# A state-space mixer and a two-layer PReLU block on one core: chunk pair 1 in the half-partition layout, and another order in the first pairs and for the rows of the second half

## The chip, the core and the metric

The kernel runs on one core of one Trainium2 chip. A core has a matrix engine (TensorE, PE in the profile, with its weight loads as PEld), three engines for elementwise work (VectorE or DVE, ScalarE or ACT, GpSimd or POOL) and queues that issue transfers between the chip's outer memory and its inner one (here nearly all from SyncE's queue, SP). TensorE writes into eight banks of a small accumulation memory (PSUM); DVE and ACT can read those banks, POOL can't. The metric is the time of one execution in device microseconds; lower is better.

## The reference

A state-space layer (four batches, eight heads, 768 tokens, head size 32, state size 16) is followed by a two-layer block with PReLU. Cut to what matters:

```python
# for each batch and head, over chunks of the sequence (the result doesn't depend on the chunk's length)
cum = np.cumsum(log(clip(a)))                       # within the chunk
L   = exp(cum[i] - cum[j]) for i >= j, else 0
y   = ((C @ B.T) * L) @ x + (C @ state) * exp(cum)[:, None]
state = exp(sum(log a)) * state + (B * exp(cum[-1] - cum)[:, None]).T @ x
# then, on all 4 x 768 = 3072 tokens, with the heads side by side (256 wide)
h = y @ w_in                                        # 256 -> 2048
g = maximum(h, 0) + alpha * minimum(h, 0)
out = g @ w_out                                     # 2048 -> 256
```

The weights arrive as 64-bit floats and are turned into 32-bit ones on the chip.

## The kernel before, in words

**Chunks and pairs.** The kernel uses chunks of 128 tokens: 6 for each batch, 24 in all, worked on in 12 pairs (pair 0 is chunks 0 and 1 of batch 0, and so on). Four chunks (two pairs) make a group of 512 tokens, for which the two-layer block then runs; there are six groups.

**Two layouts.** Pairs 0 and 1 are done in `first_two` with a chunk's 128 tokens on the 128 partitions ("whole"). All later pairs put chunk k of a pair on half k of the partitions: 64 partitions hold the first 64 tokens and then the second 64 of that chunk. Since the decay matrix L is triangular, a head then needs 128 + 64 = 192 columns (`SQ`) instead of 256 for both chunks, and the matmuls run in smaller tiles of the array, more at once. The functions of this layout are `load_tokens` and `load_chunks` (loads), `turn_products` (transposes of B and C), `gram_products` (C times B), `scan_heads` (the decays), `decayed` (their product), `added` (the addition to the state), `x_products` and, inside `pair`, the products with the state. Because a chunk's state and C are needed on the other half of the partitions too, `moved_s` and `moved_c` hold copies of them moved across.

**Decays.** A decay matrix comes out of one scan on DVE for each stretch of columns: running product of the a values, with a one added at the diagonal (`ident_h`; for the half layout the bank `ident_p`, filled by `identity_bank`). For pairs 2 and later the a values are written out to memory as rows (`rows_clamp`, `rows_ends`, `rows_scan`, `rows_product`, `rows_out`), 96 rows for each half of the batches, and read back spread over the partitions (`load_spread`, tile `abc`). For pairs 0 and 1 the a values are spread on the chip, by matmuls with a column of the identity: `spread_rows` for pair 0 and `spread` for pair 1 (64x128 tiles), into the four PSUM banks `bank(0)` to `bank(3)`. `first_a` clamps them into the tile `z`.

**Weights.** Each matrix comes in eight pieces of 512 KB; the sixteen pieces are converted in the order in0, in1, in2, out0, in3, out1, in4 and so on. A conversion is: two steps on ACT (L263, and L270 or L273), one on POOL (L265), two on DVE (`sign` L284, L294) and one on POOL (L316). `convert_a` issues the ACT steps and L265, `convert_next` the rest. At most six raw pieces are held, so a load waits for an earlier piece's end.

**The first group** runs while the weights arrive. `hidden_two` does the first two pieces of w_in as soon as pair 0 and then pair 1 are done (L968), and from f = 4 to 15 `hidden` (L953, 128 hidden features by 512 tokens) alternates with `output` (L991). The result of a hidden product sits in one of two banks (`hp`); ACT multiplies it by alpha (L956) and DVE takes the maximum (L957), which frees the bank. Between these steps the stages of pairs 2 and 3 run (`ssm`, a generator with stages at fixed places): f = 4 to 9 has pair 2, f = 9 to 14 pair 3. Of `pair`'s stages the second calls `products_of_c` (cz on ACT, cd on POOL, then moved_c on ACT, L681), the fourth has the gram and the state.

**The order is written out by hand.** Every engine executes its instructions in the order in which the code issues them, so an instruction that waits holds up all later ones of its engine. SP's transfers too are issued in order: a, B, C and x of pair 0, a of pair 1, two weight pieces, the rows out (z, pf), pair 1's loads, weight pieces 2 and 3, pair 2's loads, weight pieces 4 and 5, abc of pair 2, then one piece for each one converted.

**The rest.** From the end of f = 15 on, the groups 1 to 5 run with seven products instead of eight for each block of two by two (`quad`, `product`, L1077 and L1052), and the remaining pairs run in between.

**What the change touches**, by line: the loads of the first pairs (`load_whole` L203, called at L225 and L851), the identity tiles (L330 to L332, `identity_bank` L387), `rows_ends` (L405), `pair_loads` (L468), `first_a` (L485), `spread` (L507), `pair` (moved_c at L680, state products at L725 to L734), `first_two` (L745 on, its own `mask`, `added`, `times`, `decays`, `outputs`), and the rows of the second half (L1289 to L1295).

Of the kernel before, what the change touches and what calls it, by code (L numbers as in the profile page):

```python
# [22 lines left out]
def kernel(  # L23
# [179 lines left out]
    def load_whole(gp):  # L203


        nat, _, xt, ap = pair_tiles(gp)
        b, c = divmod(2 * gp, CPB)
        if gp == 0:
            load_a(ap, b, c)
            load_rows(0, nc.scalar)  # L210
            nc.sync.dma_start(out=al_n, in_=moe_alpha.rearrange("(k p) -> k p", p=P))
        spans = [slice((c + k) * Q, (c + k + 1) * Q) for k in range(2)]
        for k, ts in enumerate(spans):
            for i, src in enumerate((B, C)):
                nc.sync.dma_start(out=nat[:, i, k].rearrange("p (h n) -> p h n", h=H),
                                  in_=src[b, :, ts, :].rearrange("h p n -> p h n"))
        for k, ts in enumerate(spans):
            nc.sync.dma_start(out=xt[:, k].rearrange("p (h d) -> p h d", h=H),
                              in_=x[b, :, ts, :].rearrange("h p d -> p h d"))
        if gp == 0:  # L220
            loads["a", 1] = prep.tile([P, 2 * Q], F32, name="a1")
            load_a(loads["a", 1], b, c + 2)

    al_n = const.tile([NF, P], F32, name="al_n")
    load_whole(0)  # L225
# [95 lines left out]
    def keep_warm(to, n, cols=2 * Q):  # L321

        for i in range(n):
# [6 lines left out]
    ident_h = const.tile([P, H * Q], F32, name="ident_h")  # L330
    nc.vector.tensor_copy(out=ident_h.rearrange("p (h t) -> p h t", h=H),
                          in_=ident.unsqueeze(1).to_broadcast([P, H, Q]))  # L332
# [54 lines left out]
    def identity_bank():  # L387
# [3 lines left out]
        nc.scalar.copy(out=m5_bank[0][:, HT:], in_=ident_h[:, :HT])  # L391
        for s in range(2):
            nc.scalar.copy(out=m5_bank[0][HQ:, HT:].rearrange("p (a s t) -> p s a t", a=2, s=2)[:, s],
                           in_=ident[HQ:, HQ * (1 - s) : HQ * (2 - s)].unsqueeze(1)
                           .to_broadcast([HQ, 2, HQ]))
# [9 lines left out]
    def rows_ends(i, eng=nc.vector):  # L405
        d0 = held[i]
        eng.tensor_copy(out=d0[:, Q + 1 :], in_=d0[:, HQ + 1 : Q])
# [60 lines left out]
    def pair_loads(gp):  # L468
# [6 lines left out]
        if gp >= NB:  # L475
# [9 lines left out]
    def first_a(ap, eng):  # L485

        z = prep.tile([P, 2, Q], F32, name="z", bufs=2)
        eng.memset(z[:, :, :1], 0.0)
        eng.tensor_scalar(out=z[:, :, 1:], in0=ap.rearrange("p (k t) -> p k t", k=2)[:, :, 1:],
# [17 lines left out]
    def spread(z, k, tile=lambda w: ss_tile()):  # L507

        ts = [tile(w) for w in range(2)]
        for q in range(4):  # L510
            for w in range(2):
                rs = slice(64 * w, 64 * w + 64)
                row = 64 * w + N * q
                nc.tensor.matmul(ts[w][:, q * Q : (q + 1) * Q],
                                 ident[rs, row : row + 1].to_broadcast([64, P]), z[rs, k],
                                 start=(q == 0), stop=True, tile_position=(64 * w, 0),
                                 skip_group_check=True)
        return ts
# [92 lines left out]

    def dps_of(gram):
# [8 lines left out]
    def pair(gp):  # L621
# [53 lines left out]
        def products_of_c():  # L675
            for e in range(2):
                nc.scalar.mul(cz[:, e].rearrange("p k t -> p (k t)"), ct, par[:, e : e + 1])
            nc.gpsimd.tensor_tensor(out=cd.rearrange("p k t -> p (k t)"), in0=ct, in1=pf,
                                    op=ALU.mult)
            for k, (to, frm) in enumerate(others):  # L680
# [6 lines left out]
        if fine:  # L687
            for i in range(4):
# [5 lines left out]
                if i == 3:  # L694
                    products_of_c()
                    move_states()
# [10 lines left out]
        if not fine:  # L707
# [3 lines left out]
            move_states()  # L711
        for i, r in enumerate((2, 3, 0, 1) if fine else (3, 2, 1, 0)):
# [12 lines left out]
        for i in range(2):  # L725
            for q in range(4):
                qs = slice(32 * q, 32 * q + 32)
                for k in range(2):
                    ks, w = slice(HQ * k, HQ * (k + 1)), k ^ i
                    if st[k] is not None:  # L730
                        nc.tensor.matmul(y[k][qs, w], (moved_s if i else st[k])[ks, qs],  # L731
                                         moved_c[ks] if i else cd[ks, k], start=i == 0,
                                         stop=False, tile_position=(HQ * k, 32 * q),
                                         skip_group_check=True)  # L734
# [10 lines left out]
    def first_two():  # L745
# [4 lines left out]
        dec = [work.tile([P, 2, H, Q], F32, name="dec") for i in range(2)]  # L750
        first = dec[0].rearrange("p a b t -> p (a b t)").rearrange(
# [18 lines left out]
        def gram_of(bc, cz, banks):  # L770
            gram = [t.rearrange("p (k h t) -> p k h t", k=2, h=2) for t in banks]
            for k in range(2):
                for r in range(4):
                    rs = slice(32 * r, 32 * r + 32)
                    nc.tensor.matmul(gram[r][:, k].rearrange("p h t -> p (h t)"), bc[rs, k],
                                     cz[rs, :, k], start=True, stop=True,
                                     tile_position=(32 * r, 0), skip_group_check=True)
            return gram

        def added(dps, bn, xt):  # L780
# [8 lines left out]
        def mask(sm, new, ks):  # L789
            n = ks.stop - ks.start  # L790
            nc.gpsimd.tensor_tensor(
                out=sm.rearrange("p k (g m) -> p k g m", g=2),
                in0=new[:, ks].unsqueeze(2).to_broadcast([P, n, 2, 2 * D]),
                in1=hmask.rearrange("p (g m) -> p g m", g=2).unsqueeze(1)
                .to_broadcast([P, n, 2, 2 * D]), op=ALU.mult)

        def copied(gram):
            g0 = op.tile([P, GT], F32, name="o_sb").rearrange("p (k h t) -> p k h t", k=2, h=2)
            nc.scalar.copy(out=g0, in_=gram)
            return g0  # L800

        def times(i, r, gram, eng=nc.vector):
            o = dec[1][:, :, 2 * r : 2 * r + 2] if i else by_bank[:, r]
            eng.tensor_tensor(out=o, in0=gram, in1=o, op=ALU.mult)

        def decays(k, w, t):
            ws = slice(512 * w, 512 * w + 512)
            nc.vector.tensor_tensor_scan(out=dec[1][:, k].rearrange("p h t -> p (h t)")[:, ws],
                                         data0=t, data1=ident_h[:, ws], initial=0.0,
                                         op0=ALU.mult, op1=ALU.add)  # L810

        def outputs(i, tiles, st, cd, xt, ws, warm=0):
            y = [t[:, : 2 * Q].rearrange("p (k t) -> p k t", k=2) for t in tiles]
            keep_warm(y[ws[0]].rearrange("p k t -> p (k t)"), warm)
            begun = False
            for k in range(2):
                if st[k] is None:
                    continue
                for q in range(4):
                    qs = slice(32 * q, 32 * q + 32)  # L820
                    for w in range(KC):
                        hs = slice(64 * w, 64 * w + 64)
                        nc.tensor.matmul(y[w][qs, k], st[k][hs, qs], cd[hs, k],
                                         start=not begun, stop=False,
                                         tile_position=(64 * w, 32 * q), skip_group_check=True)
                begun = True
            for w in ws:
                for k in range(2):
                    for q in range(4):
# [3 lines left out]
                                         dec[1][:, k, h] if i else by_bank[:, h // 2, k, h % 2],  # L833
                                         start=False, stop=True, tile_position=(0, 32 * q),
                                         skip_group_check=True)
                nc.scalar.copy(out=xts[0][:, w, 2 * i * Q : 2 * (i + 1) * Q],
# [561 lines left out]
```

## Time and profile before

| | |
|---|---|
| runs before: median of 7 (lowest to highest) | 363.3 us (361.7 to 363.69) |
| the profiled execution: its time, its span | 363.32 us, 361.6 us |
| busy over the span: PE, PEld, DVE | 352.7, 290.5, 233.6 us |
| busy over the span: ACT, POOL | 175.8, 209.6 us |
| mean granted clock of TensorE | 0.995 |
| transfers | 29.18 MB, 101422 packets |
| L529, decays of a head in the half layout (DVE, 128x192) | 80 x 526 ns |
| L808, decays of pair 1 (DVE, 128x512) | 4 x 1208 ns |
| L953, hidden of the first group (PE, 128x512) | 48 instructions, 22.7 us |

The 32-bit matmuls of TensorE appear as two instructions each. A matmul's busy time overlaps that of the next, so a busy PE isn't a PE at its peak. The chain of waits follows the work that ended last back to its cause; its pieces are told by the engine and line that each was spent on, and "issue" is time in which the engine waited for nothing that the profile shows. The page's chain has 86% of the span on PE.

The first 84 us are the first group and its weights; the span's slices show TensorE busy to eight tenths or more in all but the last slice (each digit is a fortieth of the span):

```profile
PE   8989999899999999999999999999999999999996
DVE  6797796778845647866656856657856634643363
ACT  3467854744455345545445545445545444443431
POOL 4586668589857847545546545537535545434521
```

### The profile page before, as it was taken

How to read it: one execution, taken by the hardware profiler on the slowest of the kernel's cores; microseconds unless marked ns; L12 is line 12 of the kernel's file. 1: busy time of each engine (PE TensorE's matmuls, PEld its weight loads, DVE VectorE, ACT ScalarE, POOL GpSimd, SP SyncE). 2: the span in 40 equal slices, each digit the busy share in tenths (PEclk: the TensorE clock that was granted, in tenths of full speed). 3: DMA queues.
4: the chain of work that ended last, by engine and by line, in shares of the span. 5: the costliest groups of instructions: out<-in, count | busy, mean ns of one | idle time of the engine just before them, and what ended most of it. 6: DMA issues, size and time to landing. Idle time of an engine off the chain costs nothing.

```text
span 361.6 us, 8061 instructions
## 1 busy us (share of the span) xinstructions
PE 352.7 (98%) x3128; PEld 290.5 (80%) x3128; DVE 233.6 (65%) x467; ACT 175.8 (49%) x399; POOL 209.6 (58%) x229
## 2 busy tenths in 40 slices
PE   8989999899999999999999999999999999999996
PEld 7766667467888788888888888888888888888884
DVE  6797796778845647866656856657856634643363
ACT  3467854744455345545445545445545444443431
POOL 4586668589857847545546545537535545434521
PEclk9899999999999999999999999999999999999999
DMA  6888979742748581401452442541001001002004
GB/s 109 166 177 206 336 123 292 109 89 49 140 98 152 93 137 21 89 2 23 86 99 31 89 88 32 94 84 29 1 4 29 0 2 29 2 1 32 0 1 87
DMA packets 101422, 29.18 MB, mean 81 GB/s; under 512 B 79928, under 2 KB 97288, under 8 KB 101384
## 3 DMA queue, kind: packets, MB, share of 16 engines
q1 hardware_dynamic: 100456, 28.43, 39.3%
q8 instruction: 24, 0.39, 0.5%
q10 hardware_dynamic: 928, 0.25, 0.3%
q14 instruction: 14, 0.11, 0.1%
HBM read 25.27 MB, written 3.39 MB: 79 GB/s over the span
## 4 chain that ended last, share of the span: by engine, by line
PE 86%; POOL 4%; DVE 4%; ACT 3%; issue 2%; POOLq 0%; ACTq 0%; DVEq 0%
PE bank L1052 33%; PE hp L1077 28%; PE ss L1077 5%; PE bank L991 4%; PE hp L953 3%; PE ss L606 2%; PE ss L586 2%; PE hp L968 2%; PE hp L324 2%; PE ss L731 1%; POOL wt L265 1%; DVE gt L957 1%; POOL w_out L316 1%; ACT wt L263 1%; POOL w_in L316 1%
## 5 line engine op out<-in xcount | busy, mean ns | idle before, releaser
L1134 POOL TENSOR_TENSOR gt<-gt 128x512 f32<-128x512 f32 x58 | 73.7, 1270 | 20.9 <-DVE gt L1062 16.1
L1052 PE MATMUL bank<-gt,w_out 128*128 128x256 f32 x320 | 83.6, 382 | 0.0
L1052 PEld LDWEIGHTS bank<-gt,w_out 128*128 128x128 f32 x320 | 60.1, 190 | 9.2 <-issue 1.0
L1124 POOL TENSOR_TENSOR gt<-gt 128x512 f32<-128x512 f32 x20 | 25.4, 1270 | 63.0 <-DVE gt L1062 53.6
L1062 DVE SCALAR_TENSOR_TENSOR gt<-hp,s_mul,gt 128x256 f32<-128x256 f32 x96 | 42.0, 479 | 29.7 <-ACT gt L1060 24.8
L1052 PE MATMUL bank<-gt,ws 128*128 128x256 f32 x240 | 59.5, 379 | 0.0
L1060 ACT ACTIVATE gt<-hp,s_alpha 128x256 f32<-128x256 f32 x96 | 40.3, 471 | 32.1 <-PE hp L1077 31.0
L1052 PEld LDWEIGHTS bank<-gt,ws 128*128 128x128 f32 x240 | 45.6, 190 | 6.2
L1077 PE MATMUL hp<-xs,w_in 128*128 128x256 f32 x160 | 41.9, 384 | 0.0
L1077 PE MATMUL hp<-xs,ws 128*128 128x256 f32 x160 | 41.1, 379 | 0.4 <-DVE gt L957 0.4
L529 DVE TENSOR_TENSOR_SCAN dec<-abc,bank 128x192 f32<-128x192 f32 x80 | 37.8, 526 | 2.7 <-DMA abc<-z 2.7
L1103 DVE TENSOR_TENSOR hp<-hp,u 128x512 f32<-128x512 f32 x20 | 14.0, 698 | 35.2 <-ACT u L1101 35.2
L1077 PEld LDWEIGHTS hp<-xs,ws 128*128 128x128 f32 x160 | 30.3, 190 | 4.9 <-POOL xs L1032 0.8
L1077 PEld LDWEIGHTS hp<-xs,w_in 128*128 128x128 f32 x160 | 29.7, 190 | 4.4
L991 PE MATMUL bank<-w_out,gt 128*128 128x256 f32 x128 | 30.8, 382 | 0.0
L991 PEld LDWEIGHTS bank<-w_out,gt 128*128 128x128 f32 x128 | 23.8, 190 | 6.5 <-issue 3.0
L1077 PE MATMUL ss<-xT,w_in 128*128 128x256 f32 x96 | 24.6, 379 | 0.0
L953 PE MATMUL hp<-xT,w_in 128*128 128x512 f32 x48 | 22.7, 596 | 0.5 <-DVE gt L957 0.4
L571 POOL TENSOR_TENSOR sm<-state,bmask 128x256 f32<-128x256 f32 (+1 forms) x10 | 6.4, 641 | 27.9 <-DVE state L644 27.9
L1092 ACT COPY m<-hp 128x512 f32<-128x512 f32 x8 | 4.7, 586 | 35.4 <-PE hp L1077 35.4
L1101 ACT COPY u<-hp 128x512 f32<-128x512 f32 x20 | 11.7, 585 | 19.9 <-PE hp L1077 19.9
L1062 DVE SCALAR_TENSOR_TENSOR gt<-c,s_mul,gt 128x256 f32<-128x256 f32 x40 | 20.8, 560 | 0.0
(197 smaller groups left out, 597.9 us busy)
## 6 DMA issues: line engine op xcount, KB each, us to landing
abc<-z SPq DMA_DIRECT2D x20, 384.0 KB
raw<-in_moe_w_in_dram SPq DMA_DIRECT2D x8, 512.0 KB
raw<-in_moe_w_out_dram SPq DMA_DIRECT2D x8, 512.0 KB
xt<-in_x_dram SPq DMA_DIRECT2D x40, 64.0 KB
out_dram<-o_sb SPq DMA_DIRECT2D x32, 64.0 KB
nat<-in_C_dram SPq DMA_DIRECT2D x24, 64.0 KB
ap<-pf SPq DMA_DIRECT2D x11, 128.0 KB
nat<-in_B_dram SPq DMA_DIRECT2D x40, 32.0 KB
```

Of the source, the lines that this page charges most:

```text
L316: eng.tensor_tensor(out=d[:, ks], in0=r[:, ks], in1=g.bitcast(U32)[:, ks], op=ALU.add)
L529: nc.vector.tensor_tensor_scan(out=dec[:, h], data0=abc[:, h * SQ : (h + 1) * SQ], data1=ident_p[0][:, :SQ], initial=0.0, op0=ALU.mult, op ...
L953: nc.tensor.matmul(hp, w_in[:, k, f * P : (f + 1) * P], xts[g][:, k], start=(k == 0), stop=(k == KC - 1))
L991: nc.tensor.matmul(pos[0][t // 2][:, t % 2], gt[:, t * Q : (t + 1) * Q], w_out[:, f], start=(f == 0 and t % 2 == 0), stop=(f == NF - 1), s ...
L1052: nc.tensor.matmul(ms[g][i][:, h], w, blocks[g, z][n][:, p], start=(q == 0 and h == 0), stop=(q == NQ - 1), skip_group_check=True)
L1060: nc.scalar.mul(o[:, p], h[:, p], s_alpha[:, fs[p]])
L1062: nc.vector.scalar_tensor_tensor(out=o[:, p], in0=h[:, p], scalar=s_mul[:, fs[p]], in1=o[:, p], op0=ALU.mult, op1=ALU.max)
L1077: nc.tensor.matmul(to[:, p], w(2 * z + p), b, start=start and p == 0, stop=True, skip_group_check=True)
L1101: nc.scalar.copy(out=u2, in_=A)
L1103: nc.vector.tensor_tensor(out=Y, in0=Y, in1=u2, op=ALU.add)
L1124: nc.gpsimd.tensor_tensor(out=tc_, in0=g22, in1=g12, op=ALU.subtract)
L1134: eng.tensor_tensor(out=o, in0=x0, in1=x1, op=ALU.subtract)
```

## The change

Pair 1 goes over to the half layout. Its loads become `load_second` (B by `load_tokens`, C by `load_chunks`, x by `load_tokens`, pf by `load_heads`: eleven transfers instead of seven). Its a values are spread by `spread_halves` in 32x64 tiles, from a `z1` of 192 columns whose last 63 are copied on ACT; its four scans take 384 columns each against a new tile `ident_b`, instead of 512 against `ident_h`, which is halved. Its transposes, gram products, additions, products with the state and with x are those of the later pairs (`turn_products`, `gram_products`, `added`, `state_products`, which is now a function, and `x_products`), with four copies on ACT for moved_c and moved_s.

The order changes in these places: in the first pairs the four warming matmuls into `hp` come before `rows_turn`; the second multiplication of pair 0 on POOL comes before the conversion of the first piece; the two warming matmuls before pair 0's outputs are gone; two scans of pair 1, instead of one, come before `convert_b` of the first piece; pair 1's additions follow its gram. `rows_ends` runs on ACT. `identity_bank` is one copy. In `pair`, for pairs 2 and 3, the copies moved_c follow the states instead of cd. The clamp, ends and scans of the second half's rows (f = 14) come right after `hidden`, before the conversions and pair stages of that step; `rows_out` stays where it was.

```diff
+    def load_second():
+        nat, _, xt, ap = pair_tiles(1)
+        load_tokens(nat[:, 0], B[0], 2 * Q)
+        load_chunks(nat[:, 1], C[0], 2 * Q)
+        load_tokens(xt, x[0], 2 * Q)
+        load_heads(ap, "pf", 0, 2)
...
-    ident_h = const.tile([P, H * Q], F32, name="ident_h")
+    ident_h = const.tile([P, 4 * Q], F32, name="ident_h")
+    ident_b = const.tile([P, 2 * SQ], F32, name="ident_b")
+    for v in range(2):
+        vs = slice(HQ * v, HQ * (v + 1))
+        o = ident_b[vs].rearrange("p (e s t) -> p e s t", e=2, t=HQ)
+        for s, f in ((slice(0, 3, 2), v), (slice(1, 2), 1 - v)):
+            n = len(range(3)[s])
+            nc.vector.tensor_copy(out=o[:, :, s], in_=ident[vs, HQ * f : HQ * (f + 1)]...)
...
-        nc.scalar.copy(out=m5_bank[0][:, HT:], in_=ident_h[:, :HT])
-        for s in range(2):
-            nc.scalar.copy(out=m5_bank[0][HQ:, HT:]..., in_=ident[HQ:, HQ * (1 - s) : HQ * (2 - s)]...)
+        nc.scalar.copy(out=m5_bank[0][:, HT : HT + SQ], in_=ident_b[:, :SQ])
...
-    def rows_ends(i, eng=nc.vector):
+    def rows_ends(i):
-        eng.tensor_copy(out=d0[:, Q + 1 :], in_=d0[:, HQ + 1 : Q])
+        nc.scalar.copy(out=d0[:, Q + 1 :], in_=d0[:, HQ + 1 : Q])
...
+    def spread_halves(z, r0):
+        ts = [bank(r0 + r) for r in range(2)]
+        for e in range(2):
+            for r in range(2):
+                rs = slice(32 * (r0 + r), 32 * (r0 + r) + 32)
+                row = 32 * (r0 + r) + N * e
+                for k in range(2):
+                    nc.tensor.matmul(ts[r][HQ * k : HQ * (k + 1), e * SQ : (e + 1) * SQ],
+                                     ident[rs, row : row + 1].to_broadcast([32, HQ]), z[rs, k],
+                                     start=e == 0, stop=True,
+                                     tile_position=(32 * (r0 + r), HQ * k), ...)
...
             nc.gpsimd.tensor_tensor(out=cd..., in0=ct, in1=pf, op=ALU.mult)
+        def move_c():
             for k, (to, frm) in enumerate(others):
                 nc.scalar.copy(out=moved_c[to], in_=cd[frm, k])
...
             states(dps)
             move_states()
+            move_c()
...
+        def scans(sp, r0):
+            for r, t in enumerate(sp):
+                nc.vector.tensor_tensor_scan(out=heads_of(dec1, r0 + r), data0=t[:, : 2 * SQ],
+                                             data1=ident_b, initial=0.0, ...)
+        def moved(name, k, t):
+            to, frm = (slice(HQ * v, HQ * (v + 1)) for v in (k, 1 - k))
+            nc.scalar.copy(out=moved_to[name][to], in_=t[frm])
...
         hp = spare()
+        keep_warm(hp, 4, Q)
         rows_turn(0, pr, hp[:, 2 * Q :])
         rows_copy(0, hp[:, 2 * Q :])
-        keep_warm(hp, 4, Q)
...
         mask(sm0[0], new[0], slice(0, 1))
         g1 = copied(gram[1])
+        nc.scalar.copy(out=z1[:, :, Q + 1 :], in_=z1[:, :, HQ + 1 : Q])
+        times(1, g1, nc.gpsimd)
         convert_a(*pieces[0])
-        times(0, 1, g1, nc.gpsimd)
...
-        sp = [spread(z1, 0, lambda w: bank(2 + w))]
-        sp.append(spread(z1, 1, bank))
+        sp = [spread_halves(z1, r0) for r0 in (2, 0)]
...
-        decays(0, 0, sp[0][0])
+        scans(sp[0], 2)
         convert_b(*pieces[0])
-        decays(0, 1, sp[0][1])
         convert_next()
-        tp = spare()
-        bc1, cz1 = turned(nat1, tp)
+        scans(sp[1], 0)
+        bc1 = turn_products(nat1, bank(2))
...
-        prelus = [hidden_two(0, 0, 0, tp)]
-        added(dps[1], bn1, xt1)
-        decays(1, 1, sp[1][1])
+        prelus = [hidden_two(0, 0, 0, spare())]
+        gram = [bank(2), bank(3), ss(), ss()]
+        gram_products(bc1, cz1, gram)
+        dps = dps_of(gram)
+        added(dps, bn1, xt1)
...
+        decayed(heads_of(dec1, 0), g0, nc.gpsimd)
+        for k in range(2):
+            moved("c", k, cd1[:, k])
+        moved("s", 0, sm0[1][:, 0])
+        moved("s", 1, sm1[:, 0])
...
-        outputs(1, (bank(0), bank(1)), (sm0[1][:, 0], sm1[:, 0]), cd1, xt1, (0, 1))
+        state_products(y, (sm0[1][:, 0], sm1[:, 0]), cd1, moved_to["s"], moved_to["c"])
+        x_products(y, xt1, dec1, (True, True))
+        for k in range(2):
+            nc.scalar.copy(out=xts[0][:, :, (2 + k) * Q : (3 + k) * Q], in_=y[k])
...
         hidden(0, f)
+        if f == 14:
+            rows_clamp(1)
+            rows_ends(1)
+            held["pr"] = rows_scan(1)
+            rows_product(1)
...
             bns[4] = pair_loads(4)
-            rows_clamp(1)
-            rows_ends(1)
-            held["pr"] = rows_scan(1)
-            rows_product(1)
             rows_out(1)
```

## The prediction

> **What bounds the kernel now.** I read the busy time by stage first: from the end of the first half's work (84.46 us) to the end, from the first full hidden step (31.86) to there, and the start in three pieces. After the time, each row has the stage's length and then the busy time of PE, PEld, DVE, ACT and POOL.
>
> ```profile
> 84.46:361.60 277.14, 273.64 (x2330) 235.46 (x2330) 169.58 (x353) 126.81 (x296) 151.04 (x154) 1.00 0.29 53
> 31.86:84.46 52.60, 51.15 (x481) 33.47 (x481) 39.71 (x72) 32.95 (x68) 38.38 (x41) 1.00 0.78 186
> 13.69:20.91 7.22, 6.03 (x106) 4.53 (x105) 7.14 (x9) 4.93 (x11) 6.20 (x7) 1.00 0.76 148
> 8.19:13.69 5.50, 3.80 (x28) 2.78 (x32) 3.00 (x3) 1.60 (x7) 2.25 (x6) 0.69 0.96 244
> ```
>
> TensorE is full after 84.46, and nothing there is changed: a microsecond saved counts if TensorE's 84.46 comes earlier. TensorE was idle 1.7 us in the last row and its clock was 0.69. The chain of waits (start, us, what) shows the start:
>
> ```profile
> 9.50 0.35 ACT prh L462 x2
> 9.84 0.04 issue
> 9.89 1.79 PE hp L324 x8
> ...
> 14.38 1.28 POOL dec L804
> 15.65 0.60 POOL sm L791
> 16.26 0.09 issue
> 16.34 0.61 POOL wt L265
> ...
> 17.74 1.15 issue
> 18.89 0.61 POOL wt L265
> 19.51 0.08 issue
> 19.59 1.27 POOL w_in L316
> ```
>
> The warming matmuls wait for ScalarE's prh copies, the gram products queue behind them, and GpSimd then carries everything to w_in (20.86). Third, ScalarE in order of time, for the middle; the last bracket is the idle time before, with what ended it:
>
> ```profile
> 33.10 0.69 ACT L263 ACTIVATE wt<-raw 128x512 f32<-128x512 f32 x1 [0.51 <-DMA raw<-in_moe_w_in_dram]
> ...
> 63.14 0.60 ACT L681 COPY moved_c<-cd 64x128 f32<-64x128 f32 x2 [3.31 <-POOL cd L678]
> 63.77 0.67 ACT L263 ACTIVATE wt<-raw 128x512 f32<-128x512 f32 x1
> 64.34 0.65 ACT L270 ACTIVATE wg<-raw 128x512 f32<-128x512 uint16 x1
> 64.90 0.67 ACT L956 ACTIVATE gt<-hp,s_alpha 128x512 f32<-128x512 f32 x1
> ```
>
> Two things bind: at 33.10 a weight has only just arrived, and at 63.14 moved_c holds ScalarE for 3.31 us while the hidden product, done on TensorE at 61.7, waits for its L956.
>
> **The start (earlier by 2 to 3 us, but not all of it usable).** keep_warm moves ahead of rows_turn, so it follows L760 at 7.71. At the full clock a 128-column instruction takes about 0.11 us (half the 0.22 of the row above), so 8 end at 8.6, the turn (0.56) at 9.1, and prh is still copied at 9.27, behind cz. The gram, which starts at 11.60 now, starts at 9.3, when cz ends. Pair 1's gram ran at full clock in 1.14 us (23.19 to 24.33); this one took 2.09. So gram ends at about 10.5 instead of 13.69.
>
> New there: z1's upper halves are copied on ScalarE, behind two o_sb copies (0.60 each) and the state copy (0.22), 0.30 by the nearest row (moved_c, 64x128). Spread therefore starts near 12.1, not straight after the additions at 10.85: 1.2 us of idle TensorE. Spread itself is 16 matmuls (32 instructions) as before, of 192 instead of 128 columns over four tiles instead of two; between the gram of the same tile shape (0.83 us at L586) and the present L514 (2.29) I take 1.6. The four scans shrink from 128x512 (1.208) to 128x384; two 128x192 rows are 2 x 0.47, so 0.94, saving 4 x 0.27 = 1.1 us of DVE. Three DVE multiplications go from 0.689 to 0.55 (L592), saving 0.4; the GpSimd one from 1.28 to about 0.96. Pair 1's gram, state and x matmuls run in half as wide tiles, between no saving and a quarter. Two warming matmuls (1.14) go. Against it: four ScalarE moves of 64x128 (4 x 0.296 = 1.2), one more bc copy (2 x 0.37 for 0.58), rows_ends on ScalarE instead of DVE (0.17), and ident_b's four small DVE copies, hidden in DVE's 0.85 us wait before L343 less what the halved ident_h (0.77) frees, at worst 0.3.
>
> GpSimd runs multiplication, mask, multiplication (1.28 + 0.61 + 1.3 to 1.8) from 11.15, two L265 (0.61 each), then w_in once DVE has done sign, two scans and L294 (0.7 + 1.9 + 0.7): near 16.1 to 17.4, instead of 20.86. Through pair 1 some of that goes: y waits for moved_s, which waits for the last mask, near 22.9, and xT then stands behind the conversion on ScalarE, near 25.7 (28.3 now). The hidden step of 31.86 could come near 29.6: **2.2 us earlier**.
>
> **What takes that back: the weight at 33.10.** SP issues without a break from 7.99 to 36, so its transfers don't come earlier because engines do. From 33.10 a GpSimd chain runs: L265, bn, L316, L265, (DVE L294), L316 to 39.91, the second output weight. The output that needs it ran at 41.14, so only **1.3 us** of the start can be used here, less whatever SP loses (call it d). SP loses something: pair 1's loads become 4 + 2 + 4 and the pf load, 11 instead of 7.
>
> ```profile
> 11.03 2.86 SPq L215 DMA_DIRECT2D nat<-in_B_dram  x1
> 13.93 0.59 SPq L215 DMA_DIRECT2D nat<-in_C_dram  x1
> 14.56 2.39 SPq L218 DMA_DIRECT2D xt<-in_x_dram  x2
> ...
> 19.37 3.64 SPq L145 DMA_DIRECT2D nat<-in_B_dram  x4
> 23.06 3.47 SPq L151 DMA_DIRECT2D nat<-in_C_dram  x2
> 26.57 2.65 SPq L145 DMA_DIRECT2D xt<-in_x_dram  x4
> ```
>
> Pair 2 has the new form: 9.85 us from 19.37 to 29.22, against 8.06 (8.89 to 16.95): d = 1.8 at most. Form by form, B took 3.64 against 3.89 and xt 2.65 against 2.39, and C's form isn't changed: d = 0 at least. I take 0.7, nearer the like-for-like rows. Term one: 1.3 - 0.7 = **0.6 us** (-0.5 to 1.3).
>
> The Trainium skill speaks against this edit: "DMA: Bandwidth & Descriptors", section Bandwidth, calls transfers under 64 KB descriptor-dominated, and B's become 32 KB. It gives 0.95 us for 64 KB and 0.68 for 4 KB; as an estimate, four more transfers at 0.68 would be d = 2.7 and the total 2.0 us less than mine. The rows of B and xt above don't show it.
>
> The other rule weighed is the clock's; first the trace. TensorE was idle from 8.19 to 9.89, and the granted clock was 0.62, 0.50, 0.50 and 0.68 in the microseconds from 10 to 14. So the 1.2 us of idle before spread may cost another such window, about 1.6 us on spread and outputs; 0.9 of it is time that the late weight wastes anyway (2.2 - 1.3), so up to 0.7 of term one. I take nothing, since 1.2 is less idle than 1.7 and the idle stretches of 0.82 and 0.6 at 20.9 and 66.4 cost no clock; -0.5 already stands as its lower end. "TensorE: Matmul & The Clock Gate", HAM oscillation, would have the clock fall only past 3.4 us of idle, and the trace has it after 1.7. By that rule the cost is nil for certain.
>
> **ScalarE's stall at 63.14.** move_c goes behind the states, two stages later. L263 then starts at 59.9, not 63.77; the L956 held until 64.90 runs at 61.7, when its product ends; DVE's L957 comes after its scans at 63.5 (65.61 now), and the gram doesn't wait for an hp bank (66.41, after 0.60 of idle). The next L957 (69.18) comes after scans, sign and L294 (1.88 + 0.4 + 0.69) at 67.2, so the hidden step of 69.98 follows gram, additions and output (0.9 + 0.4 + 1.73 from 65.13) at 68.1: **1.9 us**. It is 2.0 at most, all of the waits there, and 0.8 if only the gram's wait goes and GpSimd, whose L265 now follows cd, holds L294. Behind the moved copies (0.6) stands a conversion, before a ScalarE wait of 2.40: nothing. At 40.62 the same edit frees 1.17 us of ScalarE, where TensorE wasn't waiting; it keeps term one usable.
>
> **Rows of the second half.** At 79.83 to 83.6 DVE runs clamp, ends, two scans (0.21, 1.30, 0.77, 1.42) while L957 stands behind; TensorE waits 0.45 for it at 84.46. Ahead of the conversions these fall where DVE waits for GpSimd (1.86 before 79.22), ends goes to ScalarE: **0.45 us** (0 to 0.45). rows_out's two transfers stay in their place in SP's order, and SP, waiting 11.4 us there, sends them earlier. identity_bank is one copy for three (0.94 to about 0.35) where a weight, not ScalarE, is late: nothing.
>
> **The sum**: 0.6 + 1.9 + 0.45 = 2.95, between -0.5 + 0.8 + 0 = 0.3 and 1.3 + 2.0 + 0.45 = 3.75. The profiled execution took 363.32 (span 361.6 and 1.7 around it), the median 363.3: 360.4, own range 359.5 to 363.0.
>
> **Rivals.** *The weight doesn't bind*, because transfers come earlier too (SP's rate is set by the queue): 2.2 + 2.35 = 4.55, 358.8. For it, pair 3's loads took 8.04 for B beside weights, so the queue varies; against, 33.10 is a plain DMA wait. 0.12. *The middle gives nothing*: the freed ScalarE time is taken by GpSimd or DVE in the same chain, and only 0.6 + 0.45 is left: 362.3. For it, DVE's long row of work from 42 to 57; against, its 2.14 and 3.08 us of idle. 0.12. *Hidden anyway*: d = 1.8, 0.8 in the middle, nothing for the rows: 363.0. 0.11. *Slower, pair 1's loads clog SP*: if B's four behave like pair 3's (8.04 against 3.89), d = 4.2 + 0.3 = 4.5, the weights come 3.2 after need, 0.8 returns: 365.7. It decides from d = 3.2 (1.3 + 0.8 + 1.1). For it, SP is never idle there; against, pair 2 beside 1 MB of weights took 3.64. 0.08.
>
> **From this the numbers**: forecast 0.57. A change under 0.3% (1.1 us) isn't to be told from none. Faster: 0.57, 0.12 and 0.07 of the second rival, 0.76; same: the rest of that and most of the third, 0.15; slower 0.09. Range 358.8 to 363.0.
>
> **What would show it**: gram ends near 10.5 at full clock; w_in near 17.4; ScalarE waits over 1 us for the raw of the fourth w_in piece; raw issues 2 to 5 come 0 to 1.8 us later; no ScalarE wait for cd at about 60; no wait before the gram's hp; TensorE contiguous through the former 84.46. A second clock drop between 13.7 and 17 or a raw landing past 35 would make me wrong.

## The result, and the profile after

| | before | after |
|---|---|---|
| median (lowest to highest, runs) | 363.25 us (361.65 to 365.9, 64) | 363.33 us (361.07 to 365.5, 27) |
| ratio after to before, 95% interval | | 1.0005 [0.9993, 1.0018] |
| profiled execution: time, span, mean granted clock | 363.32, 361.6, 0.995 | 363.71, 362.0, 0.991 |

No difference that can be measured; 360.4 us had been forecast. The stages of the profile after, cut where those of before were (after each time: length, busy time of PE, PEld, DVE, ACT, POOL, granted clock, DMA share, GB/s):

```profile
8.19:10.42 2.23, 2.00 (x42) 1.34 (x40) 2.02 (x3) 1.57 (x7) 1.72 (x6) 1.00 1.04 311
10.42:17.39 6.97, 3.99 (x98) 2.29 (x87) 6.49 (x10) 4.83 (x12) 6.65 (x8) 1.00 0.80 137
17.39:33.51 16.12, 14.02 (x192) 10.10 (x193) 7.69 (x17) 8.62 (x21) 8.11 (x11) 0.79 0.71 158
33.51:84.25 50.74, 50.33 (x480) 33.38 (x480) 40.76 (x74) 32.39 (x66) 37.97 (x40) 1.00 0.83 195
84.25:361.99 277.74, 273.91 (x2330) 235.50 (x2330) 168.13 (x350) 127.15 (x296) 151.40 (x154) 1.00 0.28 52
```

The gram ends at 10.2 at full clock (13.69 before), and w_in is ready at 17.39 (20.86), as forecast. From there to the first full hidden step TensorE needs 16.12 us at a clock of 0.79, and starts it at 33.51, not at 29.6: 1.65 us *later* than before (31.86). From there to the end of the first half's work it takes 50.74 us (52.60 before): the middle gained 1.86 and gave the start's loss back. TensorE's timeline shows where the start went (start, busy us, what, and in brackets the idle time before):

```profile
11.69 0.94 PE L527 MATMUL bank<-z,ident 32*64 32x192 f32 x32 [1.09 <-ACT z L903]
...
17.44 3.68 PE L992 MATMUL hp<-xT,w_in 128*128 128x256 f32 x8 [0.77 <-POOL w_in L322]
...
22.29 1.99 PE L992 MATMUL hp<-xT,w_in 128*128 128x256 f32 x8
...
26.89 0.34 PE L620 MATMUL bank<-dec,xt 64*32 64x64 f32 x15 [1.01 <-issue]
28.01 5.30 PE L992 MATMUL hp<-xT,w_in 128*128 128x256 f32 x16 [0.78 <-ACT xT L964]
33.51 0.67 PE L977 MATMUL hp<-xT,w_in 128*128 128x512 f32 x1 [0.21 <-DVE gt L1004]
```

L992 (L968 before) is the same eight instructions of work in its first and second row, and took 3.68 and 1.99 us. The windows of 3.41 us in which this trace grants the clock say why:

```profile
10.76:14.17 3.41, 2.15 (x68) 1.36 (x68) 3.40 (x6) 2.65 (x8) 3.31 (x4) 1.00 0.84 160
14.17:17.58 3.41, 1.80 (x19) 1.06 (x18) 2.94 (x5) 2.03 (x7) 3.19 (x4) 1.00 0.75 92
17.58:21.00 3.42, 3.42 (x8) 2.25 (x8) 1.01 (x2) 0.72 (x2) 2.73 (x4) 0.50 0.77 218
...
24.41:27.82 3.41, 1.75 (x96) 1.05 (x80) 2.58 (x7) 2.38 (x6) 2.37 (x5) 1.00 0.55 57
27.82:31.24 3.42, 3.23 (x8) 2.61 (x9) 1.04 (x2) 1.72 (x4) 1.41 (x2) 0.50 0.50 76
```

Each half-clock window follows one in which TensorE was busy for 51 to 53% (1.75 and 1.80 of 3.41); the one at 63% (2.15) is followed by full clock. Before had one such window, 10.23 to 13.64, behind one with 1.71 us of work; after has two, and both lie on L992. The middle, on ScalarE:

```profile
60.01 0.69 ACT L980 ACTIVATE gt<-hp,s_alpha 128x512 f32<-128x512 f32 x1 [1.20 <-PE hp L977]
60.59 0.90 ACT L704 ACTIVATE cz<-bc,par 128x256 f32<-128x256 f32 x2
63.47 0.69 ACT L269 ACTIVATE wt<-raw 128x512 f32<-128x512 f32 x1 [1.98 <-DMA raw<-in_moe_w_in_dram]
```

The wait of 3.31 us for cd is gone; 1.98 us for a weight stands at its place. SP's queue (start, us, what):

```profile
8.54 3.39 SPq L145 DMA_DIRECT2D nat<-in_B_dram  x4
11.97 2.40 SPq L151 DMA_DIRECT2D nat<-in_C_dram  x2
14.42 2.63 SPq L145 DMA_DIRECT2D xt<-in_x_dram  x4
...
30.16 0.62 SPq L253 DMA_DIRECT2D raw<-in_moe_w_in_dram  x1
```

Pair 1's loads take 8.5 us of it (8.06 before), but they also start earlier, and pair 2's begin at nearly the same time as before (19.43 and 19.37). The fourth w_in piece is issued 0.9 us later than the 29.26 of before; nearly all of that comes in pair 2's loads, which the change leaves alone and which took 10.7 us here, 9.85 before.

### The profile page after: what moved, and what is told of

It is laid out like the page before. It is cut to its first block, busy times and chain, and to the rows that moved or that the text cites. A ratio compares the mean times of both kernels' runs of the same rounds, so it can differ in the third digit from the quotient of the medians.

```text
span 362.0 us, 8189 instructions
## 1 busy us (share of the span) xinstructions
PE 351.0 (97%) x3188; PEld 288.6 (80%) x3188; DVE 231.7 (64%) x469; ACT 177.0 (49%) x405; POOL 209.0 (58%) x229
## 4 chain that ended last, share of the span: by engine, by line
PE 90%; POOL 2%; DVE 2%; issue 1%; ACT 1%; DMA 1%; SPq 1%; POOLq 0%; DVEq 0%
PE bank L1076 33%; PE hp L1101 28%; PE bank L1015 7%; PE ss L1101 6%; PE hp L977 5%; PE ss L620 2%; PE hp L992 2%; PE ss L600 2%; PE ss L634 1%; DMA nat<-in_C_dram 1%; PE ss L579 1%; POOL dec L818 1%; PE hp L600 0%; SPq L214 0%; PE bank L620 0%
## 5 line engine op out<-in xcount | busy, mean ns | idle before, releaser
L1086 DVE SCALAR_TENSOR_TENSOR gt<-hp,s_mul,gt 128x256 f32<-128x256 f32 x96 | 42.0, 479 | 30.5 <-ACT gt L1084 26.8
L585 POOL TENSOR_TENSOR sm<-state,bmask 128x256 f32<-128x256 f32 (+1 forms) x13 | 8.2, 634 | 29.7 <-DVE state L671 27.6
L1135 DVE TENSOR_TENSOR c<-hp,m 128x512 f32<-128x512 f32 x20 | 13.8, 692 | 10.6 <-PE hp L1101 10.6
```

Of the source, the lines that this page charges most:

```text
L1086: nc.vector.scalar_tensor_tensor(out=o[:, p], in0=h[:, p], scalar=s_mul[:, fs[p]], in1=o[:, p], op0=ALU.mult, op1=ALU.max)
L1135: nc.vector.tensor_tensor(out=c22, in0=A, in1=m5, op=ALU.add)
```

## The experiments

Every ratio is to the kernel before on the same chip; in us it is the ratio's distance from 1 times 363.3.

| kernel | ratio, 95% interval | us |
|---|---|---|
| e1 before + moved copies behind the states | 0.9937 [0.9914, 0.996] | -2.3 |
| e2 before + rows of the second half | 1.0001 [0.999, 1.0012] | 0.0 |
| e3 the new start alone | 1.009 [1.0077, 1.0103] | +3.3 |
| e4 after + four warming matmuls | 1.0015 [0.9999, 1.003] | +0.5 |
| e5 before + four of pair 1's loads halved | 1.0058 [1.0035, 1.0082] | +2.1 |
| e6 e4 + weights ahead of pair 2's loads | 0.9967 [0.9947, 0.9986] | -1.2 |
| e7 after + weights ahead | 1.0031 [1.0007, 1.0055] | +1.1 |
| e8 e1 + weights ahead | 0.9929 [0.991, 0.9948] | -2.6 |
| e9 before + warming matmuls moved | 0.9969 [0.9949, 0.9989] | -1.1 |
| e10 e8 + e9 | 0.9915 [0.9884, 0.9946] | -3.1 |
| e11 e9 + e5 | 1.003 [1.0002, 1.0057] | +1.1 |
| e12 e3 + four warming matmuls | 1.0035 [1.0014, 1.0056] | +1.3 |
| e13 before, 12 weight loads left out | 0.9996 [0.9977, 1.0014] | -0.1 |
| e14 after, the same | 0.995 [0.9925, 0.9975] | -1.8 |
| e15 e4, the same | 0.9908 [0.9873, 0.9943] | -3.3 |
| e16 e1, the same | 0.9918 [0.9889, 0.9946] | -3.0 |

**The parts alone (e1 to e4).** Three theories stood: A, the new start loses to the half clock what the middle wins; B, the middle only looks better behind a later start; C, the weights, late by SP's queue, decide. e1 is, in `pair`,

```diff
-            for k, (to, frm) in enumerate(others):
-                nc.scalar.copy(out=moved_c[to], in_=cd[frm, k])
+        def move_c():
+            for k, (to, frm) in enumerate(others):
+                nc.scalar.copy(out=moved_c[to], in_=cd[frm, k])
...
             states(dps)
             move_states()
+            move_c()
```

> The kernel before with one edit: the moved_c copies of pairs 2 and 3 behind the states. Theory A (the middle edits are worth what the changed kernel's profile shows between its hidden step at 33.5 and 84.25, 1.9 us, and the new start costs as much): 361.5 to 362.2, with no ScalarE wait for cd near 60 and no TensorE wait before the gram's hp bank. Theory B (the changed kernel's middle is faster only because its start is later, so that engines and weights had time to catch up): 363.0 to 363.6, the freed ScalarE time being taken by another wait before 84.5.

2.3 us faster: B falls. ScalarE's row at the same place, in e1:

```profile
58.53 0.90 ACT L677 ACTIVATE cz<-bc,par 128x256 f32<-128x256 f32 x2
61.77 0.68 ACT L263 ACTIVATE wt<-raw 128x512 f32<-128x512 f32 x1 [2.34 <-DMA raw<-in_moe_w_in_dram]
```

No instruction there waits for cd, and a raw piece that has not landed is what now ends the wait. e2 moves the rows of the second half ahead of the conversions and `rows_ends` to ACT, as the change does; e3 is the changed kernel with e1's edit and the rows' new place undone (`rows_ends` stays on ACT).

> The kernel before with one edit: the second half's clamp, ends and scans right after the hidden step of f = 14, ends on ScalarE. Theory A: TensorE's wait of 0.45 before 84.46 goes, 362.8 to 363.1. Theory B: 363.2 to 363.6, since the next product has another wait in the same place.

> The changed kernel with the middle taken back (moved_c behind cd, rows of the second half behind the pair loads); pair 1's layout and the order of the first pairs stay. Theory A (the start alone loses what the middle wins, by two stretches of half clock): 364.6 to 365.4. Theory B (start and middle are both near nothing): 363.0 to 363.6.

The rows are worth nothing: in e2 DVE's gt no longer holds TensorE at the former 84.46, but at 81.71 it now waits 0.40 us for POOL's bn of the next pair, where it had not waited before. The new start alone costs 3.3 us (four runs). e4 puts one warming matmul each ahead of `spread_halves`, `turn_products` and the first and third `hidden_two`:

```diff
+        keep_warm(bank(2), 1, GT)
         sp = [spread_halves(z1, r0) for r0 in (2, 0)]
...
+        hp = spare()
+        keep_warm(hp, 1, GT)
-        prelus = [hidden_two(0, 0, 0, spare())]
+        prelus = [hidden_two(0, 0, 0, hp)]
```

> The changed kernel with four warming matmuls (512, 256, 512 and 512 columns) where TensorE idles: before spread_halves, before pair 1's transposes, before the first and the third hidden_two. Theory A (the half clock at 17.6 to 21.0 and 27.8 to 31.2 costs 1.7 us each and comes from TensorE's idling in the 3.4 us before): granted clock 1.0 in both stretches, the first hidden_two 2.0 us instead of 3.7, the full hidden step near 31, and 360.6 to 361.8. Theory C (the weight at SP's queue decides, d = 0.9): the hidden steps come earlier but the first outputs wait for weights, 362.8 to 363.5. If the fills delay the chain itself: over 363.5.

The clock was 1.0 throughout and the hidden step came at 30.5 (33.5), and yet no time was won. ScalarE in that execution, the slowest of its twelve (365.12):

```profile
35.20 0.71 ACT L269 ACTIVATE wt<-raw 128x512 f32<-128x512 f32 x1 [4.08 <-DMA raw<-in_moe_w_in_dram]
...
43.71 0.69 ACT L269 ACTIVATE wt<-raw 128x512 f32<-128x512 f32 x1 [2.93 <-DMA raw<-in_moe_w_in_dram]
```

TensorE in the same execution:

```profile
39.17 1.98 PE L981 MATMUL hp<-xT,w_in 128*128 128x512 f32 x4 [1.15 <-POOL w_in L322]
42.06 1.99 PE L1019 MATMUL bank<-w_out,gt 128*128 128x256 f32 x8 [0.91 <-POOL w_out L322]
```

The earlier start ran into weights that were not there. The profiles before and after have no wait of TensorE for a weight from the hidden step on. A alone does not explain the result.

**The loads and their order (e5 to e8).** e5 issues pair 1's two B and two x loads in halves of 64 partitions (B's are 64 KB each; x's are 128 KB, not 64 as the expectation has it); e6, e7 and e8 move a weight pair:

```diff
-        load_next(2)
+        load_next(4)
         load_pair(2, False)
-        load_next(2)
```

> The kernel before, with the four 64 KB loads of pair 1's B and x (two of B, two of x) each issued as two halves of 64 partitions: the same bytes in the same places, four more issues on SyncE's queue, as many as the change has there. Nothing else. Theory C (the weights, pushed back by pair 1's loads, bind): raw of the fourth piece of w_in lands 1 to 2 us after the 33.1 us of the kernel before, the first full hidden step starts as before (31.9) and the weight's chain behind it comes later; 0.5 to 2 us slower, 363.8 to 365.3. Theory A (the clock alone): SyncE's queue has the issues beside its other waiting, under 0.4 us, 363.0 to 363.7. A loss with the raw landing unmoved would speak against both.

> The changed kernel with the four warming matmuls of the earlier run (no half clock there, hidden step at 30.5, weights late by 4.1, 2.9 and 0.9 us) and, besides, the fourth and fifth pieces of the weights issued ahead of pair 2's loads. Theory C: with the weights no longer behind pair 2's loads, TensorE's waits of 1.15 for w_in at 39.2 and 0.91 for w_out at 42.1 go, the hidden step stays near 30.5, and what the start gains arrives: 360.3 to 362.3, if pair 2's data, now later by the two pieces (some 3 us), isn't what its gram then waits for. Theory A (the clock alone, weights beside): the clock is already full here, so the order of the loads gives nothing, 363.4 to 364. Theory B (the start is worth nothing wherever it comes): the same, 363.4 to 364.

> The changed kernel as it is, with only the fourth and fifth pieces of the weights issued ahead of pair 2's loads. The half-clock stretches stay, so the first full hidden step stays near 33.5. Theory A: the weights aren't late against so late a start (TensorE had no wait for a weight there), 363.0 to 363.8. Theory C in its strong form (weights bind even now): 361 to 362.5.

> The kernel before with the move of moved_c behind the states (alone 361.05) and the fourth and fifth pieces ahead of pair 2's loads. In the kernel with the move alone ScalarE waits 1.7, 0.9 and 2.3 us for raw pieces at 33.5, 40.7 and 61.8. Theory C: these waits shrink and 0.5 to 1.3 us come back, 359.8 to 360.6. Theory A: the start of the kernel before is slow by its own chain up to 31.9, the weights only just keep up and their waits are covered: 360.7 to 361.4. Pair 2 too late would show as a slower run with a TensorE wait ahead of its gram.

Four more issues of the same bytes cost 2.1 us. How they cost it, e5's profile doesn't show: pair 1's loads took 9.55 us of SP's queue (8.06 before), but ScalarE converted the fourth w_in piece at 33.71 behind a wait for DVE's gt and not for the piece, TensorE waited for no weight, and it passed the end of the first half's work only 0.6 us later. That late weights are the way from these loads to the time is C's reading; e5 alone leaves it open. On the changed kernel neither remedy helps alone, weights ahead (e7, +1.1) or full clock (e4, +0.5); with both (e6) it is 1.2 us under the kernel before. The shifted weights have a price in e7: 3.4 us of clock are lost per run on the average instead of 1.9, and its three runs at full clock had a median of 362.4, the other nine 364.4. Why the clock falls there more often was not traced; the profiled execution is one of the three. On e1 the shift adds little (e8).

**The start by itself (e9 to e12).** e9 only moves the four warming matmuls ahead of `rows_turn`; e10 adds this to e8, e11 to e5; e12 is e3 with e4's warming matmuls.

> The kernel before with only the four warming matmuls put ahead of the turn of the rows, as the change has them: gram and all behind it come about 2 us earlier, no load is touched, so SyncE's queue and the weights stay where they were. The prediction's step (1.3 us of an earlier start are usable before the second output weight decides): 361.8 to 362.3. Theory C in its strict form (TensorE already runs as the weights land, no slack in the kernel before): 362.9 to 363.6, with ScalarE's wait for raw of the fourth piece longer by what the start gained. If a half-clock stretch eats it instead (theory A), the profile has one where TensorE works through pair 1.

> The kernel before with the warming matmuls ahead of the turn, moved_c behind the states, and the fourth and fifth pieces of the weights ahead of pair 2's loads; pair 1 keeps its tiles and its seven loads. Theory C: an earlier start counts here, since the weights have come forward with it and no extra loads push them: 0.7 to 1.8 us under the same kernel without the moved warming matmuls (360.7), 358.9 to 360.0. Theory B (the start is worth nothing wherever it comes): 360.4 to 361.1.

> The kernel before with both: the warming matmuls ahead of the turn (alone 1.0 us faster) and pair 1's B and x loads each in two halves (alone 2.1 us slower). If the two add, TensorE and the loads being separate lines of work: 364.1 to 364.6. Theory C (behind late weights an earlier TensorE is worth nothing): the gain of the warming matmuls goes, 365.0 to 365.8, and ScalarE waits 4 us or more for raw of the fourth piece. Under the first, some 2 us of the 3.3 that the whole new start costs are left for pair 1's new form itself; under the second, about 1.

> The changed kernel with moved_c and the rows of the second half as before (366.47 without more), and the four warming matmuls that kept the clock full in the changed kernel. Theory A (the new start costs its 3.3 us through the half clock): 364.2 to 365.2. Theory C (late weights cost it, whatever the clock): 366.0 to 367.0, at a clock of 1.0 and with ScalarE's waits for raw as long or longer.

e9 gains 1.1 us, near the 1.3 of the prediction. In its profiled execution, the slowest of its twelve, the full hidden step comes 3.1 us earlier (28.75), and TensorE then waits 1.65 us for w_in and 0.92 for w_out. What the median gains may be the clock's: e9 lost 0.33 us of clock per run on the average (1.9 before), and those runs of the kernel before that lost under 1.2 us had a median of 362.40, where e9 has 362.33. An earlier chain and a fuller clock are not told apart here. In e11 this gain and the loads' loss seem to add (+1.1, where -1.1 + 2.1 = 1.0), which speaks against the strict form of C (+1.7 or more), though the interval reaches to +2.1. e12 takes 2.0 us off e3: so much of the new start's 3.3 is the half clock, and the 1.3 left is about the 1.1 of e11. But 1.3 less e1's 2.3 would put e4 at -1.0, and it stood at +0.5. e10 is the lowest ratio with all the work done, though not told apart from e8.

**Without late weights (e13 to e16).** What hid e1's gain in e4? From the fifth weight tile on nothing is loaded:

```diff
     def load_weights(dst, src, sg):
...
+        kept.append(id(dst))
+        if len(kept) > 4:
+            raws[id(dst)] = last[len(kept) % 2]
+            return
         raw = wld.tile([P, 2, WQ, 2], U32, name="raw")
+        last[len(kept) % 2] = raw
```

> The kernel before, but from the fifth weight tile on nothing is loaded: every later piece of w_in and w_out is converted from the third or fourth tile's raw data, so the output is computed with other weights, by the same instructions; 12 loads of 512 KB are left out. No weight can be late any more. Theory C (weights bind in the kernel before too): 360 to 362. Theory A (they have slack there): 362.5 to 363.5.

> The changed kernel with the same 12 loads of weights left out (later pieces converted from the third or fourth tile's raw data). Theory C: late weights were what held the change back, so it now stands 2.5 us or more under the kernel before without these loads, near the forecast's 2.95. Theory A (half clock and the new start's own chain): 1 us or less under it; the start is still held up, and only the moved copies' gain less what the start costs is left.

> The changed kernel with the four warming matmuls and the 12 loads left out. Theory C: as the changed kernel without these loads or up to 1 us under it. Theory A: 1.5 to 3 us under it, since only now the clock is full. If it isn't under it and neither is under the kernel before without these loads, it is the new start's own chain, and both theories fall.

> The kernel before with moved_c behind the states (2.3 us faster with all loads) and the 12 loads left out. If the gain of this edit is ScalarE's stall for cd and nothing else, it stays: 1.5 to 2.5 us under the kernel before without these loads. If it came of the conversions that ScalarE gets to sooner, it shrinks to under 1 us, since no conversion is then late.

The kernel before gains nothing (-0.1), the changed one about 2.0 (1.0005 to 0.995), e4 3.9 (1.0015 to 0.9908). Late weights are thus no cost before and some 2 us after, if the loads left out stand for the weights alone: without them SP's queue is also freer for the later pairs' loads, and no run separates the two. TensorE's waits point to the weights: in the profiles of e3, e4, e9, e11 and e12 it waits, from about 36 to 42 us, 0.5 to 1.7 us for w_in and 0.9 for w_out, in those of e13 to e16 for neither. And with no weight late and the clock full (e15), the changed kernel stands where the moved copies alone do (e16): -3.3 and -3.0. The new start brings nothing that the intervals show; with six runs each they are over 2 us wide, so a microsecond either way is not excluded. The profiled executions of e13 and e14 both had a full clock, and show little gain too. The kernel before without the loads, TensorE:

```profile
18.91 1.99 PE L974 MATMUL hp<-xT,w_in 128*128 128x256 f32 x8 [0.83 <-POOL w_in L322]
...
22.27 1.99 PE L974 MATMUL hp<-xT,w_in 128*128 128x256 f32 x8
24.19 0.67 PE L829 MATMUL bank<-cd,sm 64*32 64x128 f32 x32
24.79 1.08 PE L837 MATMUL bank<-dec,xt 128*32 128x128 f32 x32
25.93 3.79 PE L974 MATMUL hp<-xT,w_in 128*128 128x256 f32 x16
29.86 1.95 PE L959 MATMUL hp<-xT,w_in 128*128 128x512 f32 x4
```

The changed kernel without them:

```profile
17.89 1.99 PE L998 MATMUL hp<-xT,w_in 128*128 128x256 f32 x8 [1.26 <-POOL w_in L328]
...
21.06 1.99 PE L998 MATMUL hp<-xT,w_in 128*128 128x256 f32 x8
...
23.71 1.31 PE L626 MATMUL bank<-dec,xt 64*32 64x128 f32 x64
25.80 3.72 PE L998 MATMUL hp<-xT,w_in 128*128 128x256 f32 x16 [0.77 <-ACT xT L970]
29.72 1.96 PE L983 MATMUL hp<-xT,w_in 128*128 128x512 f32 x4 [0.20 <-DVE gt L1010]
```

The first two products of w_in come 1.0 and 1.2 us earlier. Then pair 1's x products take 1.31 us instead of 1.08 (1.05 in e12 and e15, so not because of their tiles), and the product behind them waits 0.77 us for ScalarE's copy of xT, which before was there in time. The full hidden step comes at 29.72 against 29.86: at equal clocks the new start is worth 0.14 us in this pair. Single executions differ by more (e16, with the start of e13 and also at full clock there, has the step at 30.40), so the figure says "little" and not a size. The moved warming matmuls by themselves are worth more; in e9's profile, at full clock:

```profile
28.75 1.96 PE L953 MATMUL hp<-xT,w_in 128*128 128x512 f32 x4 [0.21 <-DVE gt L980]
```

That is 1.1 us ahead of e13, and pair 1's new form and order, which the changed kernel has besides, gives 1.0 of it back (29.72 in e14).

## Why the prediction was wrong

**The step that failed is term one, the start,** "1.3 us usable, less d = 0.7: 0.6 us" (-0.5 to 1.3). With the middle at -2.3, the rows at nothing and the whole at +0.2, it came to a loss of 2.5 us; alone, in e3, to 3.3. Three of its numbers were off:

- *"The hidden step of 31.86 could come near 29.6: 2.2 us earlier."* 29.6 is right for a full clock (29.72 in e14), but so is 29.86 for the kernel before (e13). Most of the 2.2 us was the half-clock window of the one profiled execution, taken for a delay of the chain: before, the warming matmuls took 1.79 us and the gram 2.10, in e13 1.16 and 1.14, together 1.6 us less; in e13 the turn of the rows also came 0.44 us earlier (7.19). What the warming matmuls' new place gains at full clock, 1.1 us by e9, pair 1's new form gives back behind it, for one thing in the wait for xT; this was in the working only as "some of that goes".
- *The clock at nothing,* "since 1.2 is less idle than 1.7". The trace after has two half-clock windows, each after a window that was busy for 51 to 53%, with idle stretches of 1.01 us and less. The 1.09 us of idle before spread, the stretch that was weighed, lies in the window at 63%, and full clock followed. Over all runs the clock lost per run (one minus the granted clock, times the span) is the same, 1.9 us for both kernels (means of 114 and 28 runs): the gain at the warming matmuls was lost again behind them. The prediction named this case ("a second clock drop between 13.7 and 17"; it came at 17.58), but the sum has it at nothing. With the four warming matmuls that kept the clock full, the new start cost 2.0 us less (e12 against e3). The prediction also weighed "TensorE: Matmul & The Clock Gate", HAM oscillation, in the Trainium skill, by which the clock falls only past 3.4 us of idle; in the trace after TensorE is never idle for more than 1.09 us between 8 and 33, so the measurement decides against that reading.
- *d = 0.7.* "Form by form" the rows showed too little, because the 8.06 us of pair 1's B, C and x loads in the profiled execution were long: in the eight profiles with the loads of before they took 6.2 to 8.4 us, 7.25 on the average, in the eight with the new form 7.8 to 8.8, 8.34 on the average; d is thus about 1.1. Nor does the issue decide when a piece is there: in e9 the fourth w_in piece was issued at 27.5, not 29.3, and ScalarE had it at 34.01, not 33.10. The price in time was larger: the medians have late weights cost the changed kernel 2.0 us (e14 against it) and the kernel before nothing (e13); four halved loads alone cost 2.1 (e5). As a price the upper bound of 1.8 was the better value. "DMA: Bandwidth & Descriptors", section Bandwidth, in the Trainium skill, by which the prediction's estimate put d at 2.7, pointed the right way, though its figures were measured on transfers issued from GpSimd; e5's +2.1 [1.3, 3.0] is nearest to it, though it counts time and not the delay of a piece.

**ScalarE's stall, 1.9 us: right,** and rather small: 2.3 [1.5, 3.1] alone, 1.86 between the two profiles, 2.8 without late weights (0.9996 to 0.9918). No ScalarE wait for cd is left and the gram does not wait for hp.

**The rows, 0.45: wrong.** DVE's gt no longer holds TensorE at 84.46, but POOL's bn does 2 to 3 us ahead of it, for 0.41 us in the changed kernel (82.34): a wait took the place of the one removed.

**Of the signs to look for,** the gram at 10.5, w_in at 17.4, the raw issue 0.9 later, no wait for cd, and a full TensorE through 84.46 (50.33 of 50.74 us) came true; ScalarE's wait of over 1 us for the fourth piece did not show in the profile after, whose start was too late to meet it, and was 4.08 in e4. The rival that came nearest is "hidden anyway" (363.0), but by another way: the middle gave its full gain and the start lost it. "Pair 1's loads clog SP" named the right place, but its 4.5 us is about twice what the halved loads cost.

**What stays open.** One execution's profile can't settle the split of the start's loss: the fourth piece landed between 31.9 and 34.0 us in four executions with the same loads (e2, before, e1, e9), and that of e4 was its kernel's slowest. By medians keeping the clock full takes 2.0 us off e3 but nothing off the changed kernel until weights come earlier or go. This fits a later-of-two-limits reading: in the kernels with the moved copies and no late weights, a microsecond of lost clock goes with 0.9 to 1.2 us of time (least squares over the runs of e14, e15, e16), in the changed kernel with 0.34; in e13, where the stall for cd is still there, with 0.43. That is a correlation; how much each takes of a run was not separated further.

## What to carry to other kernels

A delay seen in one profile should be asked first whether it is the chain's or the clock's: had the stage been costed at full clock for both kernels, little would have been left of the 2.2 us (0.14 in one pair of executions). When a start is bought with more, smaller loads on the queue that also carries the weights, their price belongs in the sum: four halved loads alone cost 2.1 us here. An engine that is early may only wait for weights sooner, as TensorE did for 2.1 us in e4's profile. Of a change in several parts, the single part that ends a plain wait on a full engine's path (here two copies moved behind the states, 2.3 us) may be worth all the rest: with weights ahead it gave 0.9929 [0.991, 0.9948], better than either kernel.

## What the hardware showed that was not expected

- The granted clock changed only at steps of 3.41 us in these traces, and where the grid lay differed from run to run; a window with TensorE idle for about half of it was followed by one at 0.50 (busy 1.71, 1.75 and 1.80 us of 3.41), one with 2.15 us busy was not. The busy time alone doesn't sort them: in e5 a window with 2.36 us busy (5.42 to 8.83) was followed by 0.50. Executions of one kernel so differ in the clock they lose: before, 32 of 114 runs lost under 1.2 us and had a median of 362.40, 60 lost 1.2 to 3 us (363.34), 22 more (363.54).
- TensorE stood for 1.01 us before the last 15 of pair 1's x products (1.55 in e7), among 64 small matmuls, with no wait in the trace; what it waited for was not tried.
- The same six loads (pair 1's B, C and x as before) took 6.2 to 8.4 us on SP's queue in eight executions, and the fourth w_in piece 3.8 us (before) and 6.5 us (e9) from its issue to ScalarE's use, with ScalarE waiting for it both times.
